# Attention of three token blocks laid into the first two feed-forward blocks instead of three, with values twice in a tile

## The chip, the cores and the metric

The kernel runs on one core of a Trainium2 chip. A core has five engines that run at the same time, each with its own queue of instructions: TensorE (PE in the profile; its weight loads are shown apart as PEld), VectorE (DVE), ScalarE (ACT), GpSimd (POOL) and SyncE (SP), which here only issues DMAs. They wait for each other through semaphores, and an engine's instructions start in the order in which they were written. The metric is the device time of one execution in microseconds (us).

## The reference

One transformer layer in float32 over S = 2048 tokens of width D = 576. Attention has H = 32 query heads of width 18, and one key head and one value head that all of them share; the feed-forward part (FFN) is bilinear with F = 4608 hidden columns.

```
xn = layernorm(x)
q = xn @ wq (32 heads of 18);  k = xn @ wk;  v = xn @ wv
p = softmax(q @ k.T * 18**-0.5)          # per head, 2048 x 2048
h = x + concat(p @ v) @ wo
hn = layernorm(h)
out = h + ((hn @ w_gate) * (hn @ w_up)) @ w_down
```

## The kernel before

The tokens are cut into four blocks of 512. A large product is made in float32 quality out of faster passes: an operand is split into a high part and the rest ("split", lines 92 and 93), and high times high, high times rest and rest times high are summed in PSUM.

Attention works in *pairs* (`pair`, line 586). A pair is the scores of 128 keys against 512 tokens for two heads: two matmuls side by side on TensorE (line 606) into one of two PSUM tiles named s, and then one exponential on ScalarE over 128 x 1024 numbers (line 607) into an SBUF tile P, of which there are seven. A third pair can therefore write its scores only when the exponential of the pair two before it has read them. Two pairs, so four heads, make a *visit* of 128 keys: four matmuls that multiply P by the values V and add into the PSUM tile acc (line 611). Visits that are waiting stand in `pend`, and `flush(n)` (line 614) does the first n of them one after the other; a P tile is free again after its visit. 16 visits make one group of four heads; 8 groups make one block, so a block has 256 pairs and the whole has 1024. After the last visit of a group acc is transposed by VectorE, and `normalise` (line 636) divides by the sums and sends the heads to `ob` by DMA. When a chunk of 128 rows of `ob` is complete it is split (`chunk`, line 673), the matching rows of wo are loaded and split, and `project` (line 721) multiplies the chunk by wo: eight stages (16 or 24 matmuls in all, tile yo) over three PSUM banks, each stage added to the residual tile h by VectorE (line 737). Chunks, normalisations and projections are entries of a list, `aux`, from which `run_aux` takes one twice in every FFN tile. Residual tiles have two buffers, so that of block b + 2 is loaded only when FFN block b has written its result (`load_x`).

An FFN block takes 36 *tiles* of 128 hidden columns (`ffn`, line 917). A tile is 27 passes, each of two matmuls side by side (line 937) into the PSUM tiles pg and pu; ScalarE copies pg to g (line 955), VectorE multiplies pu by g into hf (line 959). After every second tile VectorE and ScalarE prepare sums of the two hf (`left`, lines 834 to 837, and splits to the tile `room`), and in the next tile `down` multiplies them by w_down: 42 matmuls (line 897, tile y) in 14 stages over three PSUM banks, whose results VectorE adds to h (line 900) or ScalarE copies out and GpSimd adds (lines 904 and 905). So tiles come in twos: an even one with `down` and an odd one with `left`.

Block 0's attention, and the projections of queries for all blocks, come ahead of the FFN. The pairs of the later three blocks are laid between the passes of the FFN. The whole order is written out by hand; no scheduler moves it. In a tile with attention (`on`) a pair stands ahead of every fourth pass and one more after the copy to g, eight in a tile; the four visits that these make stand in one flush after the tile's passes, ahead of `down`. FFN block b may work on attention up to block b + 2 (`more(b + 2)`). In a tile without attention the passes write a tile gu out of the s banks, and `down` follows directly after the passes.

Of the kernel before, what the change touches and what calls it, by code (L numbers as in the profile page):

```python
# [26 lines left out]
P = 128  # L27
S, D, H, DH, F = 2048, 576, 32, 18, 4608
TB = 512
NB = S // TB  # L30
# [27 lines left out]
class Block:  # L58
# [527 lines left out]
    def pair(self):  # L586

        b, r = divmod(self.n_pair, 2 * NT * NG)
        g, r = divmod(r, 2 * NT)
        t, pr = divmod(r, 2)  # L590
        if r == 0:
            self.q = self.qt.pop((b, g))
        s_ = self.ps_s(f"s{b}_{g}_{t}_{pr}")
        p_ = self.p_tile([P, 2, TB], f"P{b}_{g}_{t}_{pr}")
        self.scores(s_, p_, self.q, t, pr)
        self.half.append(p_)
        if pr:
            self.pend.append((b, g, t, self.half))
            self.half = []
            if t >= 2:  # L600
                self.prefetch_q(b, g + 1)
        self.n_pair += 1

    def scores(self, s_, p_, q, t, pr):
# [9 lines left out]
    def flush(self, n):  # L614

        for b, g, t, Ps in self.pend[:n]:
            if t == 0:
                self.acc = self.ps_acc(b, g)
            self.values(self.acc, Ps, t)
            if t == NT - 1:  # L620
                os_ = self.os[g] = self.op.tile([P, TB], F32, tag="os", bufs=1, name=f"os{b}_{g}")
                self.dve.transpose(os_, self.acc)
                self.aux.insert(0, (self.round + 1, lambda b=b, g=g, o=os_: self.normalise(b, g, o), None))
        del self.pend[:n]
# [11 lines left out]
    def normalise(self, b, g, os_):  # L636
# [3 lines left out]
        if b and c is not None:  # L640
            self.load_wo(c)
        self.normal_heads(b, g, os_)
        del self.os[g]
        if c is not None:
            self.aux.insert(0, (self.round + (LANDING if b == 0 and c < 4 else 0), lambda: self.chunk(b, c), None))

    def normal_heads(self, b, g, os_):
# [12 lines left out]
        turned = ob[:, 4 if b == 0 or g < NG - 1 else 0]  # L660
        dve.transpose(turned, os_)
# [11 lines left out]
    def chunk(self, b, c):  # L673
# [47 lines left out]
    def project(self, b, c):  # L721
# [4 lines left out]
        for s in range(NQ):  # L726
# [181 lines left out]
    def room(self):  # L908
# [6 lines left out]
        self.n_tmp = 0  # L915

    def ffn(self, b):
        pe, act, dve = self.pe, self.act, self.dve
        X, hid, todo = self.X, [], None
        for f in range(NF):  # L920
            n_ = NF * b + f
            k = f % 2
            w = self.ws.pop(n_)
            on = self.more(b + 2)
            last = f == NF - 1 and b + 1 < NB
# [6 lines left out]
            for c in range(9):  # L932
                for wk, xk in ((0, 0), (0, 1), (1, 0)):
                    if on and not last and j % 4 == 0 and self.more(b + 2):
                        self.pair()
                    for o, ps in ((0, pg), (64, pu)):
                        pe.matmul(ps, w[o:o + 64, wk, c], X[o:o + 64, xk, c], start=(j == 0), stop=(j == 26))  # L937
                    if j == (8 if on else 2) and todo and not plain(n_ - 2):
# [16 lines left out]
            act.copy(g, pg)  # L955
# [3 lines left out]
            dve.tensor_tensor(hf, pu, g, ALU.mult)  # L959
            hid.append(hf)  # L960
            if k:
                self.left(n_ - 1, hid)
                hid = []
            self.flush(len(self.pend))
            if todo and on:
                drain(self.down(b, *todo))
                self.load_wd(self.n_wd + 7)
            if f < NF - 1:
                self.run_aux()
            todo = (f // 2,) if k else None  # L970
        if b + 1 < NB:
            both(self.spread(b + 1), self.down(b, *todo))
            self.load_wd(self.n_wd + 4)
            if b + 2 < NB:
                self.load_x(b + 2)
        else:
            drain(self.down(b, *todo))
# [91 lines left out]
    def run(self):  # L1069
# [9 lines left out]
        self.n_pair, self.half, self.pend, self.aux, self.round = 0, [], [], [], 0  # L1079
        self.tqs, self.in_m = [], False  # L1080
        self.p2, self.p_next, self.wo_from, self.due = None, -1, 10 ** 6, 0.0
        with ExitStack() as st:
# [80 lines left out]
            self.room()  # L1163
            self.load_wd(WD_BUFS)
            for b in range(NB):
                self.ffn(b)


RATE = 2.3
P_BUFS = 6  # L1170

# [129 lines left out]
```

## Time and profile before

| | |
|---|---|
| time, median of 3 runs | 2300.42 us (2300.23 to 2303.99) |
| span of the profiled execution | 2301.0 us |
| PE busy | 2267.3 us, 99% |
| ACT busy | 1431.8 us, 62% |
| DVE busy | 1158.8 us, 50% |
| POOL busy | 647.9 us, 28% |
| FFN block 0, first pass at | 380.7 us |
| FFN blocks 1, 2, 3, first pass at | 931.7, 1480.5, 1965.3 us |
| last tile with pairs begins at | 1811.4 us |

For the profiled execution the trace gives its span alone; it lies 0.6 us above the median of the runs. Matmuls are pipelined, so that "busy" on PE does not tell whether it runs at its best rate; what tells it is the distance from one matmul's start to the next. In the chain views a row is a start, a length that is this distance, and what stood on the chain; "x2" behind it counts matmuls. In rows of groups and of the timeline the line of the code follows (L611 is line 611), then the tile that is written, an arrow and the tiles that are read.

### The profile page before, as it was taken

To read this page: it belongs to the slowest core of one execution; us is meant where nothing else is said; L and a number is where in the kernel's file an instruction comes from. 1 tells how busy PE (TensorE), PEld (TensorE's weight loads), DVE (VectorE), ACT (ScalarE), POOL (GpSimd) and SP (SyncE) were. 2 spreads that over 40 slices of the span, in tenths; PEclk is the share of its full clock that TensorE was granted. 3 is DMA by queue.
4 is the path that set the end of the run, shared out by engine and by line. 5 is a ranking of instruction groups with operands and counts; after the bars stand their busy time and mean duration, and the time that the engine had idled before them with its cause. 6 is when DMAs were issued, how large, how long until landed. Compare 5 with 4: busy or idle time off the path is not lost.

```text
span 2301.0 us, 45837 instructions
## 1 busy us (share of the span) xinstructions
PE 2267.3 (99%) x18102; PEld 1605.8 (70%) x18102; DVE 1158.8 (50%) x2047; ACT 1431.8 (62%) x1868; POOL 647.9 (28%) x802
## 2 busy tenths in 40 slices
PE   7999999999999999999999999999999999999999
PEld 5333335777677777777777777776777788888888
DVE  7555635444444445444444445444444476556665
ACT  6889877767776765667776766577776622223322
POOL 5445400222122222222222222212222233333333
PEclk9999999999999999999999999999999999999999
DMA  5778943433344343533343343633343345655553
GB/s 176 232 256 286 300 171 93 123 104 117 116 125 130 119 133 117 189 103 120 112 128 120 118 137 114 191 96 125 124 130 106 123 165 182 202 181 170 171 173 127
DMA packets 158287, 345.38 MB, mean 150 GB/s; under 512 B 16845, under 2 KB 48461, under 8 KB 158069
## 3 DMA queue, kind: packets, MB, share of 16 engines
q1 hardware_dynamic: 155333, 331.16, 44.6%
q0 software_dynamic: 2736, 11.26, 1.6%
q8 instruction: 144, 2.36, 0.4%
q14 instruction: 74, 0.61, 0.1%
HBM read 272.45 MB, written 55.67 MB: 143 GB/s over the span
## 4 chain that ended last, share of the span: by engine, by line
PE 82%; DVE 2%; DMA 2%; ACT 1%; issue 0%; SPq 0%; POOL 0%; DVEq 0%; ACTq 0%
PE pg L937 21%; PE y L897 17%; PE acc L611 15%; PE gu L937 12%; PE s L606 9%; PE pu L937 4%; PE yo L736 3%; PE y L855 1%; DMA q<-q_dram 1%; PE ye L855 0%; DVE ws L93 0%; DMA out_dram<-h 0%; PE tx L785 0%; ACT P L607 0%; DMA X<-X 0%
## 5 line engine op out<-in xcount | busy, mean ns | idle before, releaser
L607 ACT ACTIVATE P<-s 128x1024 f32<-128x1024 f32 x1024 | 1025.5, 1027 | 285.2 <-PE s L606 204.9
L937 PE MATMUL pu<-X,ws 64*128 64x512 f32 x2565 | 693.5, 389 | 0.0
L937 PE MATMUL pg<-X,ws 64*128 64x512 f32 x2565 | 692.8, 389 | 0.0
L905 POOL TENSOR_TENSOR h<-h,tmp 128x288 f32<-128x288 f32 x408 | 317.7, 807 | 916.5 <-ACT tmp L904 915.2
L937 PEld LDWEIGHTS pg<-X,ws 64*128 64x128 f32 x2565 | 475.3, 185 | 67.8 <-DMA wdo<-wd_dram 0.8
L611 PE MATMUL acc<-P,V 128*32 128x512 f32 x4096 | 492.8, 600 | 0.7 <-ACT P L607 0.6
L937 PEld LDWEIGHTS pu<-X,ws 64*128 64x128 f32 x2565 | 472.7, 185 | 10.2
L606 PE MATMUL s<-q,kT 56*128 56x512 f32 x2048 | 439.7, 423 | 6.3 <-ACT P L607 3.8
L897 PEld LDWEIGHTS y<-wdo,room 128*128 128x128 f32 x2856 | 386.1, 188 | 49.7 <-issue 43.3
L897 PE MATMUL y<-wdo,room 128*128 128x288 f32 x2856 | 403.6, 300 | 2.3 <-DVE h L900 2.3
L904 ACT COPY tmp<-y 128x288 f32<-128x288 f32 x408 | 162.6, 399 | 326.4 <-PE y L897 321.9
L900 DVE TENSOR_TENSOR h<-h,y 128x288 f32<-128x288 f32 x544 | 234.6, 453 | 242.0 <-PE y L897 239.2
L606 PEld LDWEIGHTS s<-q,kT 56*128 56x128 f32 x2048 | 197.9, 185 | 207.0 <-ACT P L607 121.1
L937 PE MATMUL gu<-X,ws 64*128 64x512 f32 x2646 | 308.1, 389 | 0.1
L92 POOL CAST ws<-wr 128x1152 fp32r<-128x1152 f32 x144 | 167.7, 1165 | 460.5 <-PE pu L937 293.9
L611 PEld LDWEIGHTS acc<-P,V 128*32 128x32 f32 x4096 | 114.6, 109 | 248.0 <-issue 236.9
L937 PEld LDWEIGHTS gu<-X,ws 64*128 64x128 f32 x2646 | 251.9, 184 | 49.8 <-issue 4.0
L93 DVE TENSOR_TENSOR ws<-wr,ws 128x1152 fp32r<-128x1152 f32 x144 | 197.6, 1372 | 80.7 <-POOL ws L92 80.7
L959 DVE TENSOR_TENSOR hf<-pu,g 128x512 f32<-128x512 f32 x95 | 65.6, 691 | 341.2 <-ACT g L955 341.2
L93 DVE TENSOR_TENSOR room<-S,room 128x1024 fp32r<-128x1024 f32 x68 | 83.3, 1225 | 156.0 <-ACT room L92 156.0
L955 ACT COPY g<-gu 128x512 f32<-128x512 f32 x49 | 28.9, 590 | 134.5 <-PE gu L937 134.5
L92 ACT CAST room<-hf 128x256 fp32r<-128x256 f32 (+1 forms) x144 | 73.9, 513 | 46.6 <-DVE hf L959 46.4
(170 smaller groups left out, 1459.5 us busy)
## 6 DMA issues: line engine op xcount, KB each, us to landing
wdo<-wd_dram SPq DMA_DIRECT2D x492, 288.0 KB
wr<-in_wgu_dram SPq DMA_DIRECT2D x144, 576.0 KB
wd_dram<-wd_room SPq DMA_DIRECT2D x20, 1008.0 KB
q<-q_dram SPq DMA_DIRECT2D x64, 216.0 KB
q_dram<-qs SPq DMA_DIRECT2D x16, 504.0 KB
X<-X SPq DMA_DIRECT2D x28, 256.0 KB
wd_dram<-wd_hi SPq DMA_DIRECT2D x7, 1008.0 KB
wd_dram<-wd_src SPq DMA_DIRECT2D x7, 1008.0 KB
```

What stands on the lines that cost most here:

```text
L92: (copy or self.cast)(hi, src)
L93: self.dve.tensor_tensor(lo, src, f32(hi), ALU.subtract)
L606: self.pe.matmul(s_[:, i], self.kT[o:o + 56, t * P:(t + 1) * P], q[o:o + 56, pr], start=True, stop=True)
L607: self.act.activation(p_, s_, AF.Exp, scale=SCALE)
L611: self.pe.matmul(acc[32 * j:32 * j + 32, :], self.V[:, t, :], Ps[j // 2][:, j % 2, :], start=(t == 0), stop=(t == NT - 1), skip_group_chec ...
L736: pe.matmul(y[:, :HD], m, k, start=(i == 0), stop=(i == len(ms) - 1))
L897: pe.matmul(y[:, :HD], m[:, t * P:(t + 1) * P], k, start=(first and j == 0), stop=(j == 2), skip_group_check=True)
L900: dve.tensor_tensor(hs, hs, y[:, :HD], ALU.add)
L904: act.copy(z, y[:, :HD])
L905: pool.tensor_tensor(hs, hs, z, ALU.add)
L937: pe.matmul(ps, w[o:o + 64, wk, c], X[o:o + 64, xk, c], start=(j == 0), stop=(j == 26))
L959: dve.tensor_tensor(hf, pu, g, ALU.mult)
```

## The change

It changes `ffn`, `pair`, `flush`, `normalise`, `chunk` and `project`, and adds some helpers.

- Every tile of FFN blocks 0 and 1 but the last may work on attention up to the last block (`more(NB - 1)` in place of `more(b + 2)`). In the program's order this gives 12 pairs in even tiles and 10 in most odd ones (8 in some) and ends the pairs in tile 33 of FFN block 1.
- Where pairs stand is worked out while the program is written: `pace`, called ahead of every pass, puts a pair there when a count of PE's time (`t_pe`) has passed the counted end of the exponential two pairs before (`ends`), and fewer than eight P tiles are taken. The counts use the fixed times `T_PASS` to `T_DOWN`.
- Visits are flushed twice in a tile: at pass 13 (or 7, if a new group begins) and after the tile's passes (`values_due`). One flush goes up to the end of a group.
- `pace` is also called after the copy to g, and after the flush at the end of a tile, so ahead of `down`. A typical even tile is now, with the number of passes (g), pairs (s), visits (v) and matmuls of `down` (y): `g4 s g4 s g3 s g2 v2 s s g4 s g4 s g3 s g3 v3 s s y42 s s`; an odd one: `g4 s g4 s g3 s g2 v3 s s g4 s g4 s g3 s g3 v3 s s`. Before, an even one was `g4 s g4 s g4 s g4 s g4 s g4 s g3 s v4 y42 s`.
- For blocks 1 to 3 the load of wo, the split of the chunk and its projection wait in a list (`held`) until the residual tile of their block exists, and are served one chunk at a time. In the program's order the projections of block 1 stand in odd tiles of FFN block 0, those of block 2 in even tiles of FFN block 1 (after `down`), those of block 3 in tiles 1, 3, 5, 7 and 9 of FFN block 2, which have no pairs.
- The very last transposed group uses a P tile in place of a part of `ob`.

```diff
@@ pair
+        self.paced(self.n_pair)
         self.n_pair += 1
+
+    def paced(self, n):
+        self.t_pe += T_PAIR
+        if len(self.pend) * 2 + len(self.half) > P_BUFS + (self.p2 is not None):
+            self.late[n] = len(self.late)
+        else:
+            self.t_act = self.ends[n] = max(self.t_act, self.t_pe) + T_EXP
+
+    def room_for_pair(self):
+        n = self.n_pair
+        return self.more(NB - 1) and (n - 2 in self.ends and self.ends[n - 2] <= self.t_pe or n - 2 not in self.ends and n - 2 not in self.late)
+
+    def batch(self):
+        n = len(self.pend)
+        for i, x in enumerate(self.pend):
+            if x[2] == NT - 1:
+                return i + 1
+        return n
@@ flush
+        if n:
+            self.t_pe += T_SWITCH
         for b, g, t, Ps in self.pend[:n]:
+            self.t_pe += T_VISIT
+            for k in sorted(self.late)[:2]:
+                del self.late[k]
+                self.t_act = self.ends[k] = max(self.t_act, self.t_pe) + T_EXP
@@ normalise
         if b and c is not None:
-            self.load_wo(c)
+            self.held += [(b, c), (b, 4)] if c == 3 else [(b, c)]
+            self.serve()
...
-        if c is not None:
-            self.aux.insert(0, (self.round + (LANDING if b == 0 and c < 4 else 0), lambda: self.chunk(b, c), None))
+        if b == 0 and c is not None:
+            self.aux.insert(0, (self.round + (LANDING if c < 4 else 0), lambda: self.chunk(b, c), None))
@@ chunk
-        elif c == 4:
-            self.load_wo(c)
...
+    def serve(self):
+        if self.held and not self.serving and self.held[0][0] in self.h:
+            self.serving = True
+            b, c = self.held.pop(0)
+            self.load_wo(c)
+            self.aux.insert(0, (self.round, lambda: self.chunk(b, c), None))
@@ project
-        if c == 3 and b:
-            self.aux.append((self.round, lambda: self.chunk(b, 4), None))
+        if b:
+            self.serving = False
+            self.serve()
@@ ffn
+    def pace(self):
+        while self.room_for_pair() and len(self.pend) * 2 + len(self.half) < P_BUFS + 2:
+            self.pair()
+
+    def values_due(self):
+        n = self.batch()
+        if n:
+            self.flush(n)
...
-            on = self.more(b + 2)
+            on = self.more(NB - 1)
...
-                    if on and not last and j % 4 == 0 and self.more(b + 2):
-                        self.pair()
+                    if j == 7 and last:
+                        self.values_due()
+                    if on and not last:
+                        if j == 13 or j == 7 and f and self.pend and self.pend[0][2] == 0:
+                            self.values_due()
+                        self.pace()
...
-                    if j == 12:
+                    if j == 14:
                         self.run_aux(within=True)
-                    if j == 21 and b == f == 0:
-                        self.flush(len(self.pend))
...
-            if on and not last and self.more(b + 2):
-                self.pair()
+            self.t_act = max(self.t_act, self.t_pe) + 0.6
+            if on and not last:
+                self.pace()
             hf = self.hh.tile([P, TB], F32, tag="hf", bufs=2, name=f"hf{n_}")
             dve.tensor_tensor(hf, pu, g, ALU.mult)
             hid.append(hf)
+            self.values_due()
             if k:
                 self.left(n_ - 1, hid)
                 hid = []
-            self.flush(len(self.pend))
+            if on and not last:
+                self.pace()
             if todo and on:
                 drain(self.down(b, *todo))
                 self.load_wd(self.n_wd + 7)
+                self.t_pe += T_DOWN
...
+T_PASS, T_PAIR, T_VISIT, T_SWITCH, T_EXP, T_DOWN = 0.23, 0.23, 0.893, 0.2, 1.05, 5.85
```

More of the change, by code (lines that the diff above doesn't have):

```diff
@@ L659, in normal_heads @@
                           rc.unsqueeze(2).broadcast_to([P, TB // 32, DH]), ALU.mult)
-        turned = ob[:, 4 if b == 0 or g < NG - 1 else 0]
+        if b == NB - 1 and g == NG - 1:
+            turned = self.p_tile([P, TB], "turned")
+        else:
+            turned = ob[:, 4 if b == 0 or g < NG - 1 else 0]
         dve.transpose(turned, os_)
@@ L933, in ffn @@
                 for wk, xk in ((0, 0), (0, 1), (1, 0)):
-                    if on and not last and j % 4 == 0 and self.more(b + 2):
-                        self.pair()
+                    if j == 7 and last:
[4 more added lines that the diff above has]
+                        self.pace()
                     for o, ps in ((0, pg), (64, pu)):
                         pe.matmul(ps, w[o:o + 64, wk, c], X[o:o + 64, xk, c], start=(j == 0), stop=(j == 26))
+                    self.t_pe += T_PASS
                     if j == (8 if on else 2) and todo and not plain(n_ - 2):
@@ L975, in ffn @@
                 self.load_x(b + 2)
+                self.serve()
         else:
@@ L1080, in run @@
         self.tqs, self.in_m = [], False
+        self.t_pe, self.t_act, self.ends, self.late, self.held, self.serving = 0.0, 0.0, {}, {}, [], False
         self.p2, self.p_next, self.wo_from, self.due = None, -1, 10 ** 6, 0.0
@@ L1164, in run @@
             self.load_wd(WD_BUFS)
+            self.t_act = self.t_pe
+            self.ends = {n: self.t_pe for n in range(self.n_pair)}
+            self.late = {}
             for b in range(NB):
```

## The prediction

> **What bounds the kernel now.** I read the page first (busy times, slices, chain by line), then stretches of whole tiles, then the chain of waits inside a tile.
>
> ```profile
> PE 2267.3 (99%) x18102; PEld 1605.8 (70%) x18102; DVE 1158.8 (50%) x2047; ACT 1431.8 (62%) x1868; POOL 647.9 (28%) x802
> PE   7999999999999999999999999999999999999999
> ACT  6889877767776765667776766577776622223322
> PEclk9999999999999999999999999999999999999999
> PE 82%; DVE 2%; DMA 2%; ACT 1%; issue 0%; SPq 0%; POOL 0%; DVEq 0%; ACTq 0%
> ```
>
> TensorE is busy in every slice at full clock and carries the chain; ScalarE falls from 6 or 7 tenths to 2 where the pairs end. So the question is not how much ScalarE can hide but what TensorE pays for a pair. Two tiles with 16 pairs against two tiles with none tell that:
>
> ```profile
> 1047.51:1077.07 29.56, 29.56 (x248) 21.05 (x246) 11.07 (x20) 21.07 (x27) 6.91 (x8) 1.00 0.34 111
> 1077.07:1094.84 17.77, 17.77 (x147) 13.14 (x144) 8.26 (x15) 12.20 (x17) 4.08 (x6) 1.00 0.46 133
> 2015.24:2033.55 18.31, 18.31 (x153) 15.89 (x150) 11.06 (x19) 5.55 (x11) 6.94 (x8) 1.00 0.53 179
> 2027.30:2033.55 6.25, 6.25 (x56) 5.16 (x56) 2.85 (x5) 0.65 (x2) 2.05 (x3) 1.00 0.84 286
> ```
>
> Columns: length, then busy time of PE, PEld, DVE, ACT, POOL, clock, DMA. 16 pairs cost 29.56 - 18.31 = 11.25 us, 0.70 a pair; an even tile with pairs takes 17.77, an odd one 29.56 - 17.77 = 11.8. What 0.70 is made of stands in the chain at the end of an even tile and of an odd one, and at the only mid-tile flush (tile 0):
>
> ```profile
> 1055.36 0.23 PE s L606 x2
> 1055.59 3.57 PE acc L611 x32
> 1059.16 5.83 PE y L897 x42
> 1064.99 0.43 PE s L606 x2
> 1065.42 0.23 PE pg L937
> ...
> 1073.24 3.57 PE acc L611 x32
> 1076.81 0.43 PE s L606 x2
> 1077.24 0.23 PE pg L937
> ```
> ```profile
> 364.63 1.85 PE acc L611 x16
> ...
> 387.09 2.71 PE acc L611 x24
> 389.80 0.42 PE pg L937
> ```
>
> Two, three and four visits take 1.85, 2.71 and 3.57: 0.86 a visit and 0.14 once. The next instruction takes 0.42 or 0.43 instead of 0.23: a flush costs 0.14 + 0.20 = 0.34 us however few visits it has, also amid a tile. The 0.20 falls in two halves, one on leaving the old kind of work and one on starting the new (0.43 after `down` too). A pair needs 0.23 for its scores and 0.43 for its half visit, which is 0.66 of the 0.70. Only some 0.04 a pair can be saved at all.
>
> **The change, part by part.** The sum is made against the profiled span, 2301.0 us; the median of the runs lies 0.6 below it. Ahead of the FFN (380.7 us) and in FFN block 3 the order of instructions is the same in both kernels, and so are the numbers of passes, visits, `down` and projections. Moving pairs from one tile to another costs or saves nothing by itself; what changes is the seams.
>
> *Flushes.* The program's order has 94 runs of visits from the first FFN tile on, and 143 after the change: 49 x 0.34 = +16.7 us, all on TensorE's path.
>
> *Pairs ahead of `down` or a projection.* 33 doubles now stand between values and `down`, 6 between values and a projection, where values went over directly: one more seam, 39 x 0.10 = +3.9. In front of `down` their exponentials also hold ScalarE up:
>
> ```profile
> 1056.68 1.02 ACT L607 ACTIVATE P<-s 128x1024 f32<-128x1024 f32 x1 [0.41 <-PE acc L611]
> 1060.64 0.40 ACT L904 COPY tmp<-y 128x288 f32<-128x288 f32 x1 [2.94 <-PE y L897]
> 1061.46 1.21 ACT L904 COPY tmp<-y 128x288 f32<-128x288 f32 x3 [0.42 <-PE y L897]
> ```
>
> ScalarE is idle for 2.94 us before the first copy of y, which starts 1.5 after `down` (1059.16). With two exponentials queued (the first begins 0.60 after its scores, see below) ScalarE is free about 2.45 after the double's start, 1.8 after that of `down`: 0.25 later. Its bank is wanted back in the sixth of 14 stages, at 5.83 x 5/14 = 2.1, so a wait of about 0.1 is left: 33 x 0.1 = +3.3 (bounds 0 and 0.3 each).
>
> *Doubles.* The largest term. A third pair needs the first one's s tile. How long that takes stands where a double follows values before the FFN:
>
> ```profile
> 371.83 0.74 PE L606 MATMUL s<-q,kT 56*128 56x512 f32 x4
> 373.51 0.55 PE L785 MATMUL tx<-C,xh 128*128 128x128 f32 x3 [0.94 <-ACT P L607]
> ```
> ```profile
> 372.43 1.02 ACT L607 ACTIVATE P<-s 128x1024 f32<-128x1024 f32 x1 [1.64 <-PE s L606]
> ```
> ```profile
> 369.02 0.49 PE s L606 x2
> 369.51 2.39 PE acc L611 x16
> ```
>
> Exponential 0.60 after the first scores, 1.02 long, and TensorE has the tile back 373.51 - 371.83 = 1.68 after the start of the double. In the new order four passes stand between a double and the next pair: 0.34 + 0.23 + 4 x 0.23 = 1.49. So the third pair waits 0.19, and scores that had to wait take 0.49 themselves (a waiting double pays its start again), 0.10 more when a single pair amid passes needs 0.24: 0.29 each. After `down` the exponential begins some 0.05 sooner (1065.46 below, for scores at 1064.99 in the chain, whose rows start up to 0.1 after the matmul itself):
>
> ```profile
> 1065.46 2.18 ACT L607 ACTIVATE P<-s 128x1024 f32<-128x1024 f32 x2 [0.79 <-PE s L606]
> PEld s L606 <- ACT P L607: 12.1, 46, 0.4
> ```
>
> so 0.14 + 0.10 = 0.24 there. The last row (waits between 400 and 1800 us) says that scores lose only 12.1 us to ScalarE today, since single pairs come 1.15 apart. Places in the new order: 86 doubles after values with four passes and a pair behind, 27 after `down` and 4 after a projection, and 14 times a pair, one pass, a pair, three passes, a pair (due at 1.50: 0.28). 86 x 0.29 + 31 x 0.24 + 14 x 0.28 = 24.9 + 7.4 + 3.9 = +36.3. Bounds: nothing, if the exponentials come sooner, and 0.43 each, as after a full seam (+56). I take the middle because the 1.68 is the same sequence. The fourth pair doesn't wait: due at 2.9, the second exponential done at 2.6. The 150 doubles save 0.01 each against single pairs: -1.5.
>
> The Trainium skill's "TensorEngine Tiling (Array Packing)", Key Properties, says that changing the tiling mode drains TensorE; values use 32 columns, scores and passes 64 rows, so it speaks against more flushes, and the trace agrees with 0.34. It has no price; "TensorE: Matmul & The Clock Gate" (What happens when you issue a matmul) has a drain of about 128 cycles, an estimated 0.05 us at 2.4 GHz, and two for each flush would be 49 x 0.1 = 5 in place of 16.7, the sum 2359. The same page says that weight loads are pulled ahead of running matmuls; by that rule a waiting pair's weights would lie ready, its 0.10 would go, and the sum would be 13 lower; the trace speaks against it, since the row of waits names the load (PEld) itself.
>
> *Projections.* Those of blocks 1 and 2 stay beside values or `down` and cost what they do. Those of block 3 go to odd tiles without pairs, directly behind the passes, where VectorE is busy with hf and `left`:
>
> ```profile
> 1852.12 6.37 PE gu L937 x54
> ```
> ```profile
> 1859.19 0.69 DVE L959 TENSOR_TENSOR hf<-gu,g 128x512 f32<-128x512 f32 x1 [4.25 <-ACT g L955]
> 1861.63 0.68 DVE L93 TENSOR_TENSOR room<-hf,room 128x512 fp32r<-128x512 f32 x1
> 1872.13 2.99 DVE L737 TENSOR_TENSOR h<-h,yo 128x288 f32<-128x288 f32 x8
> 1876.65 0.81 DVE L107 BATCH_NORM_STATS2 bsb<-h 128x6 f32<-128x288 f32 x2
> 1883.69 0.68 DVE L959 TENSOR_TENSOR hf<-gu,g 128x512 f32<-128x512 f32 x1
> ```
>
> Passes end at 1858.49 and room at 1862.31, so the adds begin 3.8 later and go at 2.99/8 = 0.37. TensorE has three banks: its eighth stage waits for the fifth add, 3.8 + 5 x 0.37 = 5.7, and ends at 6.2. Four projections of 6.2, one of 6.0, and the statistics after the last (1876.65 to 1883.69: 7.0), which delay the next `down`: VectorE is done at 6.8 + 1.2 + 1.4 + 7.0 = 16.4 after the odd tile's passes, its first add lands at 16.9, `down` begins at 12.5 and wants it at 13.7: 3.2. Together 34.0. Today's projections of block 3 in FFN block 2:
>
> ```profile
> 1480.51:1508.11 27.60, 27.32 (x230) 19.35 (x228) 10.04 (x19) 18.26 (x21) 4.19 (x4) 1.00 0.64 204
> 1596.92:1618.32 21.40, 21.25 (x170) 16.39 (x168) 10.75 (x21) 11.69 (x16) 5.75 (x7) 1.00 0.41 131
> 1719.01:1740.40 21.39, 21.24 (x171) 16.38 (x168) 10.72 (x21) 11.69 (x16) 5.76 (x7) 1.00 0.39 130
> 1828.84:1894.62 65.78, 62.88 (x491) 53.19 (x490) 49.16 (x105) 17.11 (x35) 22.10 (x27) 1.00 0.49 162
> ```
>
> 27.60 - 2 x 11.8 = 4.0; 21.40 - 17.77 = 3.6 twice; 65.78 - 3 x 18.31 = 10.8: 22.0. Difference +12.0 (bounds 5 and 17).
>
> *The rest.* Tile 0 loses values' wait for fresh pairs (13.9 against 11.8 and one flush): -1.5. FFN block 2 opens without a pair to cover X's DMA: +0.7. Loads of wo, ob and q move on SP's queue, but each has a tile or more before its use: 0.
>
> Sum: 16.7 + 3.9 + 3.3 + 36.3 - 1.5 + 12.0 - 0.8 = +69.9, a span of 2371 and a time of 2370 us.
>
> **The rivals.** *Doubles don't wait.* If the exponential of a double starts as soon as after a single pair, 36.3 goes: 2334. For it: only 12.1 us of such waits today; against it: 1.68 in two rows.
>
> *ScalarE queues up.* Two tiles give ScalarE 21.07 us for 16 pairs, so some 27 for 22 in about 36. That isn't a bound, but if each double also made the fourth pair wait 0.2, 131 x 0.2 = 26 comes on top: 2396.
>
> *Faster.* The seam's 0.34 could belong to the end of a tile, where banks change, and not to the flush. 95 tiles with pairs become 70, saving 25 x 0.34 = 8.5, with 1.5 of tile 0: 2290. It decides only if the second flush costs under some 0.1 and doubles and projections hide; 389.80 shows the price amid a tile. That the change doesn't do what it says is excluded by the order: 12, 10 or 8 pairs a tile.
>
> **How the numbers follow.** The forecast has 0.72, doubles without a wait 0.14, ScalarE's queue 0.08, faster 0.04, no change 0.02. The range reaches from the case without waits, less 7 for projections and 3.3 for copies at their low bounds and 1 for rounding (2334 to 2323), to the queue's case, 2396, less a little. Within 0.2% (4.6 us) a measurement can't tell it from no change: faster 0.04, same 0.02, slower 0.94.
>
> **What would show it.** Two tiles with 22 pairs: 18.31 + 22 x 0.66 + 4 x 0.34 + 4 x 0.27 + 0.2, about 35.5; `PEld s <- ACT P` up from 12 to some 25 us or more; projections of block 3 near 6 us; the last pair near 1650 us. Wrong if those two tiles take 34.4 (no waits) or less (cheap flushes).

## The result, and the profile after

The changed kernel takes 2394.94 us (median of four runs, 2392.47 to 2396.82), beside 2302.2 us for the kernel before on the same chip: a ratio of 1.040, interval 1.0385 to 1.0419. The forecast, 2370 us, had the direction and most of the size; the time lies just above the upper end of the range, which the prediction puts at "2396, less a little". The profiled execution of the changed kernel has a span of 2390.7 us, 89.7 more than that of before, where the sum said 69.9. The FFN alone lost more, 93.2 us: ahead of it stand the same instructions, but this execution reaches the first pass at 377.2 us and that of before at 380.7, with a mean granted clock of 1.00 and 0.98 until then.

The page of the changed kernel, first busy times, then the slices, then the chain by engine:

```profile
PE 2335.7 (98%) x18102; PEld 1563.2 (65%) x18102; DVE 1168.8 (49%) x2047; ACT 1405.7 (59%) x1868; POOL 647.4 (27%) x802
PE   7999999999999999999999999999799999999999
ACT  6888877766776677666676777775122323233232
PEclk9999999999999999999999999999899999999999
PE 83%; DVE 2%; issue 1%; ACT 1%; DMA 0%; POOL 0%; DVEq 0%; SPq 0%; ACTq 0%; POOLq 0%
```

TensorE is still the chain, with as many instructions as before and 68 us more in them. ScalarE falls off four slices sooner than before, where the pairs end. New is one slice, the 29th, in which TensorE is busy 7 tenths and its granted clock is not full: the opening of FFN block 2. Now stretches of the changed kernel: two typical tiles, then the first two tiles of FFN block 2 and the fourth (length, busy PE, PEld, DVE, ACT, POOL, clock, DMA share, GB/s):

```profile
1501.26:1536.85 35.59, 35.53 (x284) 21.75 (x282) 13.36 (x26) 26.08 (x33) 6.87 (x8) 1.00 0.31 96
```
```profile
1672.70:1683.75 11.05, 8.75 (x55) 6.11 (x56) 1.96 (x2) 0.92 (x2) 1.89 (x2) 0.88 1.03 288
1683.75:1704.17 20.42, 13.22 (x81) 10.98 (x78) 10.54 (x17) 3.24 (x5) 3.38 (x3) 0.75 0.54 195
```
```profile
1716.75:1729.39 12.64, 10.02 (x79) 8.26 (x78) 9.84 (x19) 2.90 (x5) 3.73 (x5) 1.00 0.51 172
```

Two tiles with 22 pairs take 35.59 us at full clock, where 35.5 was forecast. The fourth tile of FFN block 2, an odd one with a projection, takes 12.64, so 6.4 above an odd tile without one (6.25), near the 6.2 of the forecast. But the first tile takes 11.05 and the second 20.42, where the sum had 6.9 and some 12.4. From the first pass up to FFN block 2 the changed kernel lost 65.8 us (forecast 57.2). FFN block 2's first eleven tiles take 147.2; the same tiles without pairs and projections take 97.8 in the kernel before (six of 6.25 and five of 12.06) and its projections of block 3 cost 22.0, so 27.4 are lost there (forecast 12.7).

The chain of the changed kernel at the end of an even tile, in rows of start, length and work:

```profile
1477.84 2.71 PE acc L633 x24
1480.55 0.66 PE s L628 x4
1481.22 6.03 PE y L936 x42
1487.24 0.66 PE s L628 x4
1487.90 0.23 PE pg L991
...
1488.82 0.50 PE s L628 x2
```
```profile
PEld s L628 <- ACT P L629: 66.4, 152, 0.8
```

Three visits still take 2.71 (the trace has eight instructions for a visit's four matmuls). The double ahead of `down` takes 0.66, `down` 6.03 in place of 5.83, and the third pair behind the next double 0.50. The last row is the group of waits between 400 and 1660 us (their sum, how many, the longest): scores lose 66.4 us to ScalarE's exponentials, in the kernel before 10.8 in this window.

Then the timeline at the opening of FFN block 2 (start, busy time, engine, operation, output and input, count, and in brackets the idle time ahead and what ended it):

```profile
1663.29 6.72 SPq L702 DMA_DIRECT2D ob<-turned  x9
...
1670.11 6.70 SPq L836 DMA_DIRECT2D X<-X  x8
...
1672.67 4.15 PE L991 MATMUL gu<-X,ws 64*128 64x512 f32 x33
...
1676.90 3.19 SPq L928 DMA_DIRECT2D out_dram<-h  x4
...
1678.21 1.64 PE L991 MATMUL gu<-X,ws 64*128 64x512 f32 x10 [1.40 <-DMA X<-X]
1680.49 0.50 PE L991 MATMUL gu<-X,ws 64*128 64x512 f32 x1 [0.64 <-DMA X<-X]
1681.25 9.38 PE L991 MATMUL gu<-X,ws 64*128 64x512 f32 x64 [0.26 <-DMA X<-X]
...
1684.75 1.76 SPq L1040 DMA_DIRECT2D h<-in_x_dram  x4
1686.55 0.43 SPq L736 DMA_DIRECT2D wor<-in_wo_dram  x1
...
1692.14 0.67 POOL L92 CAST wos<-wor 128x576 fp32r<-128x576 f32 x1 [16.95 <-DMA wor<-in_wo_dram]
...
1692.87 0.53 PE L774 MATMUL yo<-wos,room 128*128 128x288 f32 x2 [2.23 <-POOL wos L92]
...
1694.57 1.91 PE L774 MATMUL yo<-wos,room 128*128 128x288 f32 x7 [1.17 <-DVE wos L93]
```

SyncE issues the nine DMAs of the last normalisation (`ob<-turned`) for 6.72 us, and only then those of X, which the passes of the new block read; TensorE stands for 1.40, 0.64 and 0.26 us. Behind X come the result, w_down and the residual tile, and wo is asked for only at 1686.55: its load waits for the residual tile by the rule of the new list. The first projection starts 2.23 us late, and waits again for VectorE.

### The profile page after: what moved, and what is told of

Read it like the earlier page. It is cut to its first block, busy times and chain, and to the rows that moved or that the text cites. A ratio compares the mean times of both kernels' runs of the same rounds, so it can differ in the third digit from the quotient of the medians.

```text
span 2390.7 us, 46004 instructions
## 1 busy us (share of the span) xinstructions
PE 2335.7 (98%) x18102; PEld 1563.2 (65%) x18102; DVE 1168.8 (49%) x2047; ACT 1405.7 (59%) x1868; POOL 647.4 (27%) x802
## 4 chain that ended last, share of the span: by engine, by line
PE 83%; DVE 2%; issue 1%; ACT 1%; DMA 0%; POOL 0%; DVEq 0%; SPq 0%; ACTq 0%; POOLq 0%
PE gu L991 19%; PE pg L991 17%; PE y L936 17%; PE acc L633 15%; PE s L628 11%; PE yo L774 3%; PE pu L991 1%; PE y L894 1%; ACT P L629 1%; DVE room L93 0%; PE ye L894 0%; DVE hf L1013 0%; ACT g L1008 0%; DMA q<-q_dram 0%; DVE ws L93 0%
## 5 line engine op out<-in xcount | busy, mean ns | idle before, releaser
L629 ACT ACTIVATE P<-s 128x1024 f32<-128x1024 f32 x1024 | 992.3, 1027 | 337.1 <-PE s L628 290.1
L991 PE MATMUL pu<-X,ws 64*128 64x512 f32 x1890 | 524.0, 390 | 0.0
L991 PE MATMUL pg<-X,ws 64*128 64x512 f32 x1890 | 523.9, 390 | 0.0
L991 PE MATMUL gu<-X,ws 64*128 64x512 f32 x3996 | 470.7, 391 | 3.3 <-DMA X<-X 2.3
L991 PEld LDWEIGHTS gu<-X,ws 64*128 64x128 f32 x3996 | 382.7, 185 | 81.4 <-issue 8.4
L628 PEld LDWEIGHTS s<-q,kT 56*128 56x128 f32 x2048 | 183.3, 184 | 328.0 <-ACT P L629 177.5
L991 PEld LDWEIGHTS pg<-X,ws 64*128 64x128 f32 x1890 | 350.0, 186 | 69.8 <-issue 2.0
L991 PEld LDWEIGHTS pu<-X,ws 64*128 64x128 f32 x1890 | 350.0, 186 | 3.0 <-DVE hf L1013 0.2
L1013 DVE TENSOR_TENSOR hf<-pu,g 128x512 f32<-128x512 f32 x70 | 48.4, 692 | 434.0 <-ACT g L1008 434.0
L1008 ACT COPY g<-gu 128x512 f32<-128x512 f32 x74 | 43.7, 590 | 197.8 <-PE gu L991 197.8
```

The costliest lines, as they stand in the source:

```text
L628: self.pe.matmul(s_[:, i], self.kT[o:o + 56, t * P:(t + 1) * P], q[o:o + 56, pr], start=True, stop=True)
L629: self.act.activation(p_, s_, AF.Exp, scale=SCALE)
```

## The experiments

The theory is that of the prediction, with two parts more that the trace of the changed kernel showed, (5) and (6): (1) a flush costs 0.34; (2) a third pair behind a double and four passes costs 0.24 to 0.29 more; (3) a double ahead of `down` costs a seam and late copies; (4) projections in odd tiles without pairs wait for VectorE; (5) X is late because of SyncE's queue; (6) wo is late because it is asked for late. The main rivals are that doubles do not wait, that a flush amid a tile is cheap, and that the opening is bound by the bandwidth of the DMA engines.

**One pass more behind a double, in the changed kernel.** The new flag `seam` is set by a flush and by `down`.

```diff
-            self.t_act = self.ends[n] = max(self.t_act, self.t_pe) + T_EXP
+            self.t_act = max(self.t_act, self.t_pe) + T_EXP
+            self.ends[n] = self.t_act + (0.2 if self.seam else 0.0)
+        self.seam = False
...
+            self.seam = True
...
+                self.seam = True
```

> The changed kernel, with the first pair after values or after `down` counted as ending 0.2 us later, so that five passes instead of four stand between a double and the next pair. Flushes (143), doubles, tiles with pairs and all work are the same. Theory (the third pair waits for the first one's exponential, 0.29 us after values and 0.24 after `down` or a projection): 117 such waits go and the 14 places with one pass between two pairs stay, so about 0.28 x 117 = 33 us less than the changed kernel, some 2362 us; in the rows of waits, scores behind ScalarE fall from 66 us to about 25 or less between 400 and 1660 us. Rival (the doubles do not wait, the 66 us of waits are covered by work that TensorE still has in its pipeline): within 5 us of the changed kernel, 2390 to 2398.

Measured 2374.03 us, ratio to before 1.031 (1.0293 to 1.0327): 21 less than the changed kernel. Two tiles, and the row of waits:

```profile
1485.88:1520.73 34.85, 34.85 (x284) 21.48 (x282) 13.28 (x25) 25.80 (x33) 6.87 (x8) 1.00 0.32 99
```
```profile
PEld s L630 <- ACT P L631: 51.6, 213, 0.8
```

The rival is out: the doubles do wait. But 21 us went and not 33, only 0.18 for each of the 117 places. In the traces a third pair after values costs 0.28 us more than a pair that waits for nothing before this edit and 0.06 behind it, one after `down` or a projection 0.24 and 0.02: 32 us before, 6 behind. Of these 26 some 2 come back in pairs that now follow another after three passes (246, before 138), which cost 0.03 each; the rest isn't assigned. The waits are recorded more often and are shorter, 0.24 us each instead of 0.44, and their row did not fall as far as expected.

**The same wait, put into the kernel before.** Two pairs at pass 0, the third at pass 4 or at pass 5, the rest at 12, 16, 20, 24:

```diff
-                    if on and not last and j % 4 == 0 and self.more(b + 2):
-                        self.pair()
+                    for _ in range({0: 2, 4: 1, 12: 1, 16: 1, 20: 1, 24: 1}.get(j, 0)):
+                        if on and not last and self.more(b + 2):
+                            self.pair()
```

> The kernel before, with its eight pairs a tile at passes 0, 0, 4, 12, 16, 20, 24 and after the copy to g: a double directly after values or after `down`, and four passes before the third pair. One flush a tile as before, same tiles. Theory (the third pair waits 0.29 us after values, 0.24 after `down`): some 94 x 0.27 = 25 us over the kernel before, about 2327 us. Rival (doubles do not wait): within 5 us of it, 2298 to 2307 us.

> As the kernel with a double and four passes before the third pair, but with five passes: pairs at passes 0, 0, 5, 12, 16, 20, 24 and after the copy to g. Theory (the third pair needs the s tile 1.68 us after the double's start; five passes make it due at 1.72): no wait, within 3 us of the kernel before, 2299 to 2306 us; so 25 us between this kernel and the one with four passes. If doubles cost something else than this wait (a start of their own, ScalarE queued up), this one lies over the kernel before by the same 20 us or more as the one with four passes. Rival (doubles do not wait): both the same as the kernel before.

Measured 2321.00 us (ratio 1.0082, 1.0065 to 1.0098) with four passes and 2300.25 (0.9996, 0.9986 to 1.0005) with five. Two tiles of each, first with four passes, then with five:

```profile
1056.35:1086.36 30.01, 29.98 (x249) 20.52 (x246) 11.16 (x20) 21.02 (x27) 6.90 (x8) 1.00 0.34 109
```
```profile
1046.05:1075.60 29.55, 29.55 (x249) 20.76 (x246) 11.14 (x20) 20.91 (x27) 6.91 (x8) 1.00 0.35 111
```

Third pairs behind two doubles in two tiles cost 30.01 - 29.55 = 0.46, 0.23 each, and a pass more takes it all away. A double as such costs nothing; the place of the third pair does. This is the cleanest pair of runs of the study.

**A second flush in the kernel before, without doubles.**

```diff
...
+                    if on and not last and j == 16 and not b == f == 0:
+                        self.flush(self.batch())
...
-            self.flush(len(self.pend))
+            keep = 1 if on and f < NF - 2 and self.more(b + 2) else 0
+            self.flush(max(0, min(self.batch(), len(self.pend) - keep)) if keep else len(self.pend))
```

> The kernel before, with values flushed a second time in each tile with pairs, at pass 16, and nothing else: eight single pairs a tile, no doubles, the same 95 tiles. Theory (a flush costs 0.34 us wherever it stands): about 92 x 0.34 = 31 us over the kernel before, some 2333 us, and two tiles with 16 pairs take 29.56 + 0.68 = 30.2 us. Rival (the 0.34 belongs to the end of a tile, where the banks change, and a flush amid passes costs under 0.1): at most 8 us over it, 2302 to 2310 us.

Measured 2350.32 us (1.0209, 1.0192 to 1.0226), 50 over the kernel before, with 91 more flushes in the trace. Two tiles of FFN block 0:

```profile
528.30:558.45 30.15, 30.15 (x248) 20.38 (x245) 10.85 (x18) 20.32 (x26) 6.92 (x8) 1.00 0.37 113
```

30.15 against 29.56 is 0.30 a flush; in FFN block 1 two tiles take 30.4, which is 0.42. So the price of 0.34 stands and the rival's "under 0.1" falls. The total is 19 us above 91 x 0.34. Of these 12 are projections: their share of TensorE's time in FFN blocks 0 to 2 (from the start of each of their matmuls to that of the next) is 65.6 us, 53.9 before. The edit moved them, so the run isn't as clean as its expectation says: since a visit is kept over, a group of heads ends half a tile later, and eight projections of FFN blocks 0 and 2 went from even tiles, behind `down`, to odd ones, where the seven of 24 matmuls take 5.2 to 5.3 us instead of 3.7 to 3.9. (Those of FFN block 1 went the other way and take 0.3 more each.) In odd tiles of the kernel before a projection takes 3.4; there four visits (3.57 us) stand between the passes and it, here one (1.00), so that VectorE has less time to catch up. The other 7 us are not assigned. So a second flush has a price of its own, and another that depends on what the values covered.

**Doubles ahead of `down`.** First in the kernel before, two pairs ahead of `down` instead of at passes 0 and 4 behind it; then the changed kernel without its pairs there:

```diff
-                    if on and not last and j % 4 == 0 and self.more(b + 2):
+                    if on and not last and j % 4 == 0 and self.more(b + 2) and not (j < 5 and k and f > 1):
...
+            if todo and on and f < NF - 2:
+                for _ in range(2):
+                    if self.more(b + 2):
+                        self.pair()
             if todo and on:
```

> The kernel before, with two of its pairs ahead of `down` instead of at passes 0 and 4 behind it, in some 43 tiles; one flush a tile, no pair near behind the double, so that no third pair waits. Theory (a double ahead of `down` costs 0.10 us for its seam and 0.19 for the copies of y that ScalarE's two exponentials hold up): 43 x 0.29 = 12 us over the kernel before, some 2313 us, with `down` at 6.04 instead of 5.85. Rival (the seam is only moved, and the copies have slack): within 4 us of the kernel before.

```diff
-            if on and not last:
+            if on and not last and not todo:
                 self.pace()
             if todo and on:
```

> The changed kernel without the pairs ahead of `down`: ten pairs in a typical even tile instead of twelve, so the pairs end in tile 3 of FFN block 2 and block 3's projections fall into even tiles. What is told apart is the price of a double ahead of `down`, read from a typical even tile, 20.8 us before the edit: two pairs at 0.66 less and 0.20 (the price of the prediction) give 19.3 us, with 0.40 (0.20 for two seams, 0.19 for the copies of y) 19.1, with the 0.57 of the kernel before with two pairs ahead of `down` 18.95. Time: 16 us less for projections in even tiles, about 8 less since pairs cover the opening of FFN block 2, 33 times the price less, and 5 flushes more: 2365 us at 0.20, 2358 at 0.40, 2353 at 0.57.

The first takes 2325.36 us (1.0101, 1.0086 to 1.0117): 24 over the kernel before for 42 doubles, 0.57 each, twice the 0.29 that was expected. Its chain, and two tiles of the other run:

```profile
1067.89 0.65 PE s L606 x4
1068.54 6.03 PE y L897 x42
1074.57 0.43 PE pg L937
```
```profile
1376.48:1410.35 33.87, 33.83 (x274) 21.17 (x271) 12.59 (x24) 24.26 (x31) 6.91 (x8) 1.00 0.33 101
```

`down` takes 6.03 (5.83 before): 0.20, which covers the copies. The double takes 0.65, as one pair with a seam (0.43) and one without (0.23), so what the pair behind `down` paid is paid here; and the first pass behind `down` now takes 0.43 instead of 0.23: a whole seam, 0.20 and not 0.10. That names 0.40 of the 0.57. In most of the odd tiles behind, the rest can be seen in the trace: the row of 0.43 is a single matmul, whose pu starts 0.22 behind it (1074.50 and 1074.72), and the passes stay out of step by one matmul until the end of the tile, where one slot more of 0.23 is needed. In the changed kernel, where a pair and not a pass follows `down`, that doesn't occur. No run tests it. In the changed kernel two tiles go from 35.59 to 33.87 with two pairs (0.23 each) and one visit (0.86) fewer: 1.72 - 1.32 = 0.40 for the double. The chain of the changed kernel, quoted above, says the same: 0.66 for two pairs that amid passes take 0.46, and 0.20 for `down`. So it costs 0.40 there, not 0.20.

The time of the second run, 2374.22 us (1.032, 1.0304 to 1.0336), is above all three forecasts, and the fault lies in these: its trace has 163 flushes, 20 more than the changed kernel and not 5, and 150 third pairs behind four passes instead of 117, since the count places all other pairs anew. 20 x 0.34 + 33 x 0.28 = 16 us come back that way, which is about the distance to the forecast for 0.40, 2358. The even tile that was to tell the prices apart was no fair measure either, as its odd partner lost a visit; the two tiles together are.

**Block 3's projections in even tiles of FFN block 2.**

```diff
-                         lambda: b in self.h and (c in self.wos if b else self.n_pair >= self.wo_from)))
+                         lambda: b in self.h and not self.odd_off and (c in self.wos if b else self.n_pair >= self.wo_from)))
...
+            self.odd_off = k == 1 and not on
...
```

> The changed kernel, with block 3's projections kept out of the odd tiles of FFN block 2, so that they stand in even ones, behind `down`, as those of the kernel before did. Theory (in odd tiles a projection waits for VectorE's sums of hf, and the first one for the late wo): five projections at about 4 us instead of 6 to 11, 15 to 25 us less than the changed kernel, 2370 to 2380 us. Rival (the place does not matter, and VectorE or the load of wo holds them there too): within 5 us of the changed kernel.

Measured 2378.84 us (1.0349, 1.0332 to 1.0366), 16 less. An even and an odd tile there, and in the changed kernel; the last row is an odd tile and the next even one of the changed kernel:

```profile
1721.38:1743.44 22.06, 21.90 (x176) 19.49 (x174) 15.80 (x29) 6.18 (x12) 7.73 (x9) 1.00 0.47 161
```
```profile
1729.39:1755.30 25.91, 23.29 (x175) 19.89 (x174) 16.64 (x30) 6.16 (x12) 7.53 (x9) 0.95 0.43 137
1716.75:1741.59 24.84, 22.22 (x177) 18.93 (x176) 16.33 (x30) 6.18 (x13) 7.48 (x10) 1.00 0.46 147
```

The same work takes 22.06 or 25.91 us, with VectorE busy for about as long (15.80 and 16.64). Some 1.1 of the difference goes with the granted clock, 0.95: at full clock the same work in the changed kernel takes 24.84. For the other 2.8 what counts is whether `down` stands between VectorE's sums and the projection.

**The opening of FFN block 2.** Three kernels: the last normalisation half a tile later; wo of block 3's first projection early; both.

```diff
-                self.aux.insert(0, (self.round + 1, lambda b=b, g=g, o=os_: self.normalise(b, g, o), None))
+                self.aux.insert(0, (self.round + (2 if b == NB - 1 and g == NG - 1 else 1), lambda b=b, g=g, o=os_: self.normalise(b, g, o), None))
```
```diff
-        if self.held and not self.serving and self.held[0][0] in self.h:
+        if self.held and not self.serving:
+            first = self.held[0] == (NB - 1, 0)
+            if not first or not self.early:
+                if first or self.held[0][0] in self.h:
+                    self.load_wo(self.held[0][1])
+                    self.early = first
+        if self.held and not self.serving and self.held[0][0] in self.h:
             self.serving = True
             b, c = self.held.pop(0)
-            self.load_wo(c)
...
```

> The changed kernel, with the normalisation of the very last group of heads one entry of the list later (half a tile), so that the loads of X for FFN block 2 stand ahead of its DMAs in SP's queue instead of behind them. Theory (X lands late because SP waits in front of it for VectorE's transposes; TensorE then stands in the first tile of FFN block 2): the first tile of FFN block 2 falls from 11.1 us to about 6.5, and the time by 4 to 10 us, to 2385 to 2391; what wo costs in the next tile stays. Rival (X is held up by the DMA engines' bandwidth, whatever the order of issue): the first tile stays within 1 us of 11.1 and the time within 2 us of the changed kernel.

> The changed kernel, with the rows of wo for block 3's first projection loaded and split as soon as those of block 2 are used up, many tiles before FFN block 2, in place of behind the burst of loads that opens it. Everything else stays. Theory (the first projection waits for wo, and VectorE with it, 2.23 + 1.17 + 3.80 us in the rows of waits): the second tile of FFN block 2 falls from 20.4 to about 13 to 14 us, and the time by 6 to 8, to some 2388 us; the first tile keeps its 11.1. Rival (VectorE's work and the burst of DMAs hold the projection there whatever wo does): the second tile stays above 18 us and the time within 3 us of the changed kernel.

> The changed kernel with both edits at the opening of FFN block 2: wo early, and the last normalisation half a tile later, so that X's loads come first in SP's queue. Theory (two separate waits, and the half clock that follows them): first tile about 7 us, second about 13, time 10 to 13 us under the changed kernel, some 2383 us; no slice at less than full clock there. Rival (one takes the other's place): not under 2388 us.

With the normalisation later: 2392.52 us (1.0402, 1.0385 to 1.042), 2.4 less than the changed kernel, which the runs can hardly tell from nothing and is less than the 4 to 10 expected. The first tile does what the theory says:

```profile
1673.38:1680.32 6.94, 6.51 (x54) 5.55 (x55) 1.96 (x2) 0.92 (x2) 1.90 (x2) 1.00 1.03 287
```

6.94 in place of 11.05 at the same share of DMA: it was the order in SyncE's queue, not the bandwidth. But 0.5 us of the 4.1 are lost again by the end of the block; the second tile, still without wo, takes 20.67.

With wo early: 2375.12 us (1.0316, 1.0302 to 1.033), 20 less, three times what was expected, and for another reason. The first projection now stands in the first tile and not in the second, so all the others have moved to even tiles: 16 of the 20 are the gain of the run above. This edit does not tell the wait for wo apart. With both: 2383.59 us (1.0357, 1.0343 to 1.0371), 11 less, as expected (10 to 13); here the projections stay in odd tiles, the first two tiles of FFN block 2 take 7.06 and 14.70 us, and the two waits are shown to be separate costs: wo alone is worth 20.67 - 14.70 = 6.0 in the second tile. That the clock would be full there was wrong: the second tile has 0.83.

**The edits together.** Five passes behind a double, projections in even tiles, normalisation later; and the same with wo early:

> The changed kernel with all three edits together: five passes behind a double, block 3's projections in even tiles of FFN block 2, the last normalisation half a tile later. Theory (the three costs are separate and add): 33 + 20 + 6 = about 59 us less than the changed kernel, some 2336 us, and still some 30 us over the kernel before, for 49 more flushes (16.7), the copies of y behind doubles (6.3), the seams of doubles (3.9) and what the 14 places with one pass between pairs and the irregular tiles cost. Rival (they are one cost, that only moves): less than 40 us, over 2355 us.

> All four edits: five passes behind a double, block 3's projections in even tiles, last normalisation half a tile later, wo early. From the kernel with three of them (2357.0 us), by the theory that the wait for wo costs some 5 us there (4.87 + 1.60 us of waits for ws behind wos, and half clock behind them): about 2351 us. Still about 50 us over the kernel before, which are then the flushes (16.7), doubles ahead of `down` (10), what is left of third and fourth pairs' waits (some 15), the irregular tiles and the opening. Rival (the burst of DMAs itself bounds the opening): 2357 us as without it.

2357.01 us (1.0251, 1.0234 to 1.0268) and 2347.66 (1.0199, 1.0185 to 1.0213). The first is 38 under the changed kernel, and the three runs alone give 21 + 16 + 2 = 39: the costs add, though each of them was smaller than forecast. By its number alone the run falls on the rival's side (less than 40 us, over 2355); what speaks against the rival is the sum of the three. The second takes another 9. Its first two tiles of FFN block 2 show an opening without a wait, at full clock, with the DMA engines busy throughout:

```profile
1655.21:1661.61 6.40, 6.40 (x54) 5.13 (x55) 1.96 (x2) 0.92 (x2) 1.89 (x2) 1.00 1.03 271
1661.62:1667.76 6.14, 6.14 (x58) 5.07 (x55) 3.60 (x6) 0.99 (x2) 1.15 (x1) 1.00 1.03 375
```

What is left is 46 us over the kernel before. Flushes (16.7), doubles ahead of `down` or a projection (14) and what third pairs still cost (6) name 37 of it; the rest isn't assigned, and no run shows whether another order would take more away.

**A version that beats both.** The kernel before, with two small waits taken away:

```diff
-                    if on and not last and j % 4 == 0 and self.more(b + 2):
+                    if on and not last and (j in (0, 4, 8, 13, 17, 21, 25) if k == 0 and f else j % 4 == 0) and self.more(b + 2):
...
-                self.aux.append((self.round, lambda: self.all_statistics(b), None))
+                if b == NB - 1:
+                    for s in range(NQ):
+                        self.aux.append((self.round, lambda s=s: self.statistics(b, s), None))
+                    self.aux.append((self.round, lambda: self.finish(b), None))
+                else:
+                    self.aux.append((self.round, lambda: self.all_statistics(b), None))
...
```

> The kernel before with two small edits that the traces point to: in even tiles the pairs at passes 12, 16, 20, 24 stand one pass later (the pair at pass 20 now waits 0.11 us for ScalarE, some 41 times: 4.5 us), and the last statistics, which hold VectorE for 7 us and cost 1.8 us of `down` (7.61 for 5.85), are taken in four parts. Theory (both are waits that nothing takes over): 4 to 6 us under the kernel before, some 2296 us. Rival (the wait moves to the next pair, and the other entries of the list come later): within 2 us of it.

Measured 2295.22 us against 2300.94, 0.9976 (0.9967 to 0.9985).

```profile
1040.77:1070.28 29.51, 29.51 (x248) 21.82 (x246) 11.09 (x20) 21.07 (x27) 6.92 (x8) 1.00 0.35 111
```
```profile
PEld s L606 <- ACT P L607: 10.8, 41, 0.4
```
```profile
PEld s L606 <- ACT P L607: 0.6, 1, 0.6
```

These are the same two tiles as the 29.56 of the kernel before; the even one alone takes 17.65 instead of 17.75, and so do the others like it. FFN blocks 0, 1 and 2 take 2.0, 1.8 and 1.9 us less each; in the last, `down` behind the statistics takes 6.86 instead of 7.61. The last two rows are the waits of scores for ScalarE between 400 and 1660 us, first in the kernel before: 41 waits became one. Those waits are gone and nothing took their place; of the statistics' 1.8 us in `down` 1.0 is still there.

## Why the prediction was wrong, point by point

**Flushes, 16.7: right.** 49 more in the trace, 0.30 to 0.42 each by the run with a second flush. The Trainium skill's "TensorEngine Tiling (Array Packing)", Key Properties, has the drain but no price for it; the sum of 2359 that the estimated drain of 0.05 us gave falls, since that needs 0.1 a flush.

**Third pairs, 36.3: right.** The trace shows 0.28 after values and 0.24 after `down` or a projection, for 0.29 and 0.24 forecast. By the runs 0.18 to 0.23 go with one more pass. Of the 14 places with one pass between pairs only half wait, for 0.24: 86 x 0.28 + 31 x 0.24 + 7 x 0.24 = 33. The rival that doubles don't wait is excluded by three runs. The rival of ScalarE's queue is excluded too, although its time, 2396, is the nearest to the result: fourth pairs take 0.23, and with five passes a double costs nothing. A time that fits does not make the mechanism.

**Pairs ahead of `down`, 3.9 + 3.3: mis-sized.** "One more seam, 39 x 0.10" took half of a seam where a whole one, 0.20, is paid, and "a wait of about 0.1 is left" is 0.20 in `down`. At 0.40 each the 33 doubles cost 13 us and the 6 ahead of a projection, at 0.20, another 1: 14, twice the forecast. At the 0.57 of the kernel before the 33 would cost 19.

**Projections of block 3 in odd tiles, 12.0: right for those that wait for VectorE alone** (6.3 each for 6.2 at full clock; 16 us less in even tiles). Those of blocks 1 and 2 cost what they did, 35.2 us for 35.1, though one of block 2 stands in an odd tile.

**"Loads of wo, ob and q move on SP's queue, but each has a tile or more before its use: 0": the step that failed.** In the program's order that is so for the lists, but wo's load waits for the residual tile, which waits for the old block's result, in tiles that without pairs last 6 us instead of 12; and the DMAs of the last normalisation stand ahead of X's. The opening "without a pair to cover X's DMA" was put at 0.7 and cost 4.8 (11.05 for 6.25) with the queue; the first projection was put at 6.2 and its tile takes 14.2 more than an odd tile without one (20.42 for 6.25) with wo. That is 4.1 and 8.0 us over the forecast; another 2.6 lie in the nine tiles behind, where the clock below has its part. FFN block 2 so has 14.7 us of the 23 by which the sum falls short of the FFN's 93.2. The runs take 4.1 of them away by X ahead of the normalisation's DMAs and 6.0 by wo early.

**The rival "faster"** needed a second flush for under 0.1; it costs 0.30 or more.

In all: flushes 16.7, third pairs 33, doubles ahead of `down` or a projection 14, FFN block 2 27.4, less the 1.5 of tile 0 as forecast: 90, beside 93.2 in the FFN of the profiled executions and 92.7 between the medians. The other 3 are not assigned. The doubles' own gain of 1.5 is not seen: with five passes behind them they leave the time as it is.

## What to carry to other kernels

When work is packed closer, price the seams, and count every change of kind in the new order in both directions: work put between two others opens a seam on either side. Then ask what the moved work had been covering where it stood: the pairs hid the loads that open a block, and with them gone a tile is half as long, so a load that was "a tile ahead" is half as far ahead. Walk the DMA queue in its order across such a place and name for each load what it waits for, above all loads that a new condition holds back.

## What the runs showed of the hardware that was not expected

A short wait of TensorE can cost more than itself. At the opening of FFN block 2 the three waits for X make 2.3 us, and the tile takes 4.1 less when X is asked for first. The granted clock of the changed kernel behind X's waits, in the stretch that follows it, and during the first projection (the columns as above; the clock stands behind POOL):

```profile
1681.87:1684.57 2.70, 2.70 (x13) 2.17 (x14) 0.00 (x0) 0.11 (x1) 0.00 (x0) 0.51 1.04 409
1684.57:1690.03 5.46, 5.46 (x51) 4.66 (x49) 0.69 (x1) 0.89 (x2) 0.00 (x0) 1.00 0.98 343
1700.27:1703.80 3.53, 3.53 (x15) 3.53 (x15) 2.28 (x6) 0.06 (x1) 0.00 (x0) 0.50 0.04 17
```

13 matmuls of passes take 2.70 us at a clock of 0.51, 0.21 each, and 51 take 5.46 at full clock, 0.107 each; 15 of the projection take 0.235 each, where 24 behind `down` take 3.72, 0.155 each. The Trainium skill's "TensorE: Matmul & The Clock Gate", Part 1 (The HAM clock gate), names a full and a half clock and an idle window of about 3.4 us before the half. The half agrees; but no single wait ahead of the first of these stretches was longer than 1.40 us: between 1676.82 and 1681.25 TensorE stood for 2.3 of 4.4 us, in three pieces with 11 matmuls in between. So here a stretch with little work was enough; how much work would have kept the clock up, no run shows. In the kernel with all four edits, where these waits are gone, the first two tiles of FFN block 2 have a clock of 1.00.
